# Short-convolution additions and the product with v issued to GpSimd instead of VectorE, with another table of order moves

## Chip, cores and metric

The kernel runs on one core of a Trainium2 chip. The metric is the device time of one launch in microseconds (us), lower is better. Engines are named as in the profile: PE (TensorE matmul), PEld (its weight loads), DVE (VectorE), ACT (ScalarE), POOL (GpSimd), SP (the queue that issues most DMAs).

## What is computed

Two kinds of layer alternate over a sequence of 2048 tokens with 640 channels, in float32. A is a gated convolution layer, B a two-matrix ReLU layer; each adds to the residual.

```python
def _A_ref(q, k, v, shift_k, ssm_k, ssm_D):
    for t in range(4):                       # short causal convolution, per channel
        k_shift = k_shift + k_pad[:, t:t + S, :] * shift_k[:, 3 - t]
    kv = k_shift * v
    y = long_causal_convolution(kv, ssm_k)   # per channel, by FFT in the reference
    return q * (y + kv * ssm_D)
x = x + _A_ref(_layernorm(x), ...)
x = x + relu(_layernorm(x) @ w1) @ w2        # 640 -> 1728 -> 640
```

The same A and B are applied twice (A, B, A, B) with the same k, v and weights, so y is computed once and used twice.

## The kernel before, in words

The sequence is cut into 8 chunks of 256 tokens. The long convolution is done chunk by chunk in a transformed domain. The work is cut into 21 units; a unit is two blocks of 128 channels (or one, for the last block of chunks 0 and 1) of one chunk or of two chunks. `transform` prepares a unit: it loads k, v and the filter, makes the four taps of the short convolution, adds them into the tile `acc`, multiplies `acc` with v (L729), forms sums and differences `sd` (L731, L732), transposes them on PE (L801) and multiplies them with a cosine matrix (tiles `pr`, `pg`). The results (`at`, `gt`) are spilled to memory for later chunks. `products` multiplies transformed chunks with transformed filters (L920 into `pd` or `pacc`, L925 adds them up), and PE transforms back (tile `pq`). The layer-norms, the residual and the two matrix products per chunk and layer are in `prep` and `main`; a main is one chunk and layer of 256 tokens, except in chunks 0 and 1, where it is half a chunk. In `main` PE makes `h` (L1461 to L1464), ACT applies the ReLU (L1604), DVE forms the low half `hl` (L1605), and PE multiplies both halves with w2 (L1433 to L1436).

The taps. In the first three units, all of chunk 0, a DVE instruction multiplies and adds in one (L708, L719). In the other 18 units ACT writes a scaled tap into a buffer `tp`, of which there are two (L651), and an addition `acc <- acc, tp` follows (L725), three times per unit. The product with v is at L729 in all 21 units.

Which engine runs an elementwise step with a name is decided by the tuple `ONPOOL`: a step whose name is in it goes to GpSimd, any other to VectorE.

```python
def gps(n, fn, reads, writes, prio):
    plan.op("POOL", 0.15 + n * 0.0021, fn, reads, writes, prio)
def ew(k, n, fn, reads, writes, prio):
    if k in ONPOOL:
        gps(n, lambda: fn(POOL), reads, writes, prio)
    else:
        dve(n, lambda: fn(DVE), reads, writes, prio)
```

The order on every engine is made ahead of time by `Plan`: a list scheduler that gives each step a cost and a priority, picks on each engine the ready step of best priority, and repeats this with keys that the table `MOVES` disturbs. What comes out is a fixed sequence per engine; on the chip each engine runs its own in order and waits where an input is late. GpSimd has little in its queue before: constants at the start, and 40 accumulating DMAs later (L673 adds `hr` to the filter tile `gs`; L786 makes the third part of `at` and `gt`).

Of the kernel before, what the change touches and what calls it, by code (L numbers as in the profile page):

```python
# [60 lines left out]
    (696239, 0.5, 108, 1308, 100), (709771, 15, 448, 848, 30), (757111, 1, 108, 118, 1000), (501689, 2, 206, 216, 1000), (793993, 2, 337, 737, 300), (75396, 2, -13, 137, 300),  # L61
    (827797, 0.2, 700, 850, 300), (811472, 0.5, -596, 604, 30), (617709, 4, 132, 532, 30), (809540, 1, 194, 594, 100), (987377, 4, 212, 362, 100), (205444, 2, 45, 195, 10),
    (511112, 2, 487, 547, 1000), (877225, 0.5, -33, 117, 300), (117084, 0.5, 145, 1345, 30), (392551, 8, -154, 246, 30), (228520, 2, 569, 969, 10), (284008, 8, -67, 1133, 10),
    (718585, 8, 678, 738, 30), (888747, 8, 287, 297, 1000), (962148, 1, -66, 1134, 30), (296808, 4, 510, 570, 300), (465037, 4, 78, 88, 1000), (771820, 0.5, 54, 114, 1000),
    (450406, 2, 321, 381, 300), (193537, 15, 214, 274, 3), (390307, 15, -131, 269, 10), (245960, 2, 317, 717, 30), (135498, 0.5, 639, 789, 300), (838399, 2, -31, 119, 30),
    (360983, 0.2, 554, 704, 1000), (762403, 4, 691, 751, 100), (938671, 8, 327, 477, 10), (89728, 4, -473, 727, 10), (53109, 4, 519, 544, 300), (356850, 0.5, 379, 779, 100),
    (50293, 0.2, -60, 1140, 300), (819375, 8, 99, 159, 30), (379115, 0.5, 382, 782, 100), (93648, 1, 680, 705, 1000), (398170, 1, 336, 486, 300), (829260, 8, 97, 497, 10),
    (707274, 15, 550, 700, 30), (415872, 0.5, -400, 800, 30), (727371, 1, 318, 378, 1000), (130652, 1, 379, 779, 30), (7433, 8, 107, 1307, 10), (559442, 4, 770, 795, 300),
    (621464, 0.2, 120, 1320, 100), (859335, 2, 72, 132, 100), (385222, 4, -58, 92, 100), (385554, 1, -208, 992, 30), (907221, 15, -2, 148, 30), (379287, 8, 337, 347, 300),
    (661111, 1, 156, 1356, 30), (909741, 4, 503, 903, 3), (697842, 1, -509, 691, 30), (89717, 0.5, 279, 339, 1000), (280960, 15, 440, 500, 100), (679836, 0.2, 571, 721, 100),  # L70
    (372502, 8, -207, 193, 30), (458612, 8, 109, 259, 30), (86548, 2, 537, 597, 300), (884426, 8, 814, 839, 30), (434125, 0.5, 499, 649, 100), (315057, 2, -68, 1132, 10),
    (730170, 4, 229, 629, 30), (126174, 0.5, -435, 765, 30), (190559, 8, 740, 750, 300), (255787, 1, 223, 373, 100), (722617, 15, 603, 753, 10), (21533, 4, 637, 787, 30),
    (280667, 1, 192, 217, 1000), (789770, 1, -605, 595, 100), (519538, 1, 274, 674, 100), (973148, 1, -605, 595, 30), (800972, 2, 392, 417, 1000), (816430, 2, 86, 236, 30),
    (391026, 4, 193, 218, 30), (486292, 2, 462, 487, 1000), (96439, 1, 408, 468, 1000), (453822, 4, 463, 613, 100), (905038, 4, -235, 965, 10), (934931, 0.5, 456, 856, 100),
    (379448, 15, 110, 135, 30), (847180, 8, 639, 789, 30), (651893, 8, 191, 341, 10), (974932, 0.2, -333, 867, 100), (898605, 8, 814, 874, 100), (328450, 0.5, 272, 332, 1000),
    (798154, 2, 143, 168, 100), (712104, 15, 472, 872, 10), (912566, 8, 568, 628, 100), (271480, 4, 37, 437, 10), (978163, 15, 327, 387, 100), (427782, 4, -183, 217, 30),
    (277854, 8, 79, 229, 30), (116122, 1, 42, 1242, 30), (253383, 0.5, -391, 809, 30), (622704, 2, 399, 459, 1000), (954265, 1, -25, 1175, 10), (867752, 8, 92, 242, 3),
    (390094, 0.2, 472, 872, 1000), (476637, 8, 573, 633, 100), (169012, 15, 299, 359, 30), (691903, 0.5, 435, 585, 1000), (646340, 0.5, -130, 1070, 30), (448317, 4, 84, 144, 100),
    (242667, 8, 722, 782, 30), (72971, 1, 737, 797, 300), (706991, 2, 238, 388, 100), (555710, 0.2, 15, 165, 1000), (9127, 1, 134, 1334, 100), (326956, 4, 177, 1377, 3),
    (307605, 1, -144, 1056, 30), (139482, 8, 303, 328, 300), (72000, 4, 291, 351, 100), (53081, 8, 129, 529, 3), (894170, 1, -58, 1142, 30), (451873, 2, 275, 675, 30),  # L80
    (115506, 15, 181, 1381, 10), (224945, 4, 48, 108, 30), (421425, 0.2, -6, 144, 1000), (381049, 4, 705, 765, 100), (497728, 1, -46, 354, 100), (543923, 8, 755, 905, 3),
    (536244, 2, 605, 755, 100), (953119, 2, 78, 138, 30), (676870, 15, 43, 68, 30), (372928, 15, -23, 377, 3), (605775, 15, 172, 182, 100), (30852, 4, 43, 1243, 10),
    (836145, 1, 121, 521, 100), (583412, 2, 508, 533, 1000), (752286, 0.2, 60, 460, 100), (353978, 15, 181, 241, 30), (607191, 15, 433, 583, 30), (874516, 4, 315, 375, 100),
    (661545, 8, -141, 259, 3), (508993, 15, 44, 194, 10), (920832, 2, 513, 913, 30), (157791, 8, 822, 882, 300), (527839, 0.5, -2, 148, 100), (376321, 1, 325, 725, 100),
    (928893, 2, 722, 782, 100), (205389, 15, 669, 729, 30), (166129, 15, 668, 1068, 10), (200362, 15, 178, 1378, 3), (552466, 4, 2, 152, 30), (763892, 0.5, 115, 140, 1000),
    (490494, 15, 597, 747, 30), (907558, 0.5, 392, 792, 30), (160270, 4, 393, 543, 100), (779627, 2, 443, 503, 300), (803556, 15, 140, 540, 10), (518039, 8, 503, 563, 100),
    (232112, 1, 122, 1322, 10), (902345, 2, -354, 846, 30), (9895, 1, 571, 631, 1000), (366264, 15, 65, 90, 30), (936527, 15, 293, 693, 3), (79619, 4, -169, 231, 30),
    (370231, 15, 518, 668, 30), (971813, 8, 488, 888, 10), (357754, 8, 312, 322, 1000), (237151, 2, 590, 740, 100), (305234, 15, 379, 404, 30), (754176, 2, 349, 749, 30),
    (418234, 8, 383, 408, 100), (105563, 1, 220, 1420, 30), (39099, 0.5, -595, 605, 30), (617760, 4, 143, 153, 300), (462015, 1, -177, 223, 100), (561869, 15, 759, 819, 3),
    (867484, 1, 491, 516, 1000), (792807, 0.5, 165, 565, 300), (893093, 8, -282, 918, 3), (961195, 0.5, 272, 422, 300), (780129, 2, 23, 48, 1000), (215859, 2, 290, 440, 100),  # L90
    (57360, 4, 427, 577, 30), (129201, 4, 623, 683, 300), (320957, 4, 316, 376, 100), (924052, 4, 450, 600, 30), (167525, 8, 361, 511, 100), (140874, 15, 265, 275, 300),
    (477116, 0.2, 95, 1295, 100), (107592, 8, 219, 279, 30), (671450, 2, 81, 106, 100), (121218, 1, -143, 1057, 30), (807461, 15, 494, 554, 100), (100199, 4, 247, 397, 30),
    (645106, 8, 479, 504, 3), (967239, 8, 249, 309, 30), (599905, 4, -178, 222, 30), (130555, 4, 339, 739, 10), (636712, 15, 594, 744, 10), (186050, 8, -324, 876, 10),
    (632646, 4, 303, 363, 100), (717447, 15, 289, 314, 100), (837830, 8, 146, 296, 3), (286728, 1, -33, 1167, 30), (513363, 4, 448, 598, 30), (515689, 15, 110, 1310, 3),
    (731992, 2, 151, 551, 30), (883402, 2, 136, 1336, 30), (375061, 15, 464, 614, 30), (475228, 2, -64, 1136, 30), (289290, 4, -475, 725, 10), (447762, 4, 122, 132, 1000),
    (889528, 0.5, 240, 1440, 100), (802878, 15, 447, 847, 10), (300829, 2, 576, 726, 100), (115977, 2, 572, 632, 300), (542977, 15, 762, 912, 10), (481545, 4, 507, 657, 100),
    (272913, 8, -107, 293, 10), (458051, 4, 302, 312, 1000), (855640, 15, 254, 314, 30), (554685, 0.5, -477, 723, 30), (873255, 4, 304, 454, 30), (247105, 4, 208, 268, 100),
    (120225, 8, 356, 506, 30), (35554, 2, 373, 398, 300), (836984, 2, -604, 596, 30), (47715, 1, -372, 828, 30), (274188, 15, -423, 777, 3), (510639, 8, 629, 779, 30),
    (422172, 1, 412, 472, 1000), (766593, 4, 276, 336, 100), (233761, 8, 6, 31, 1000), (759964, 4, 154, 1354, 30), (597972, 1, 233, 1433, 100), (191352, 0.2, 195, 345, 1000),
    (703329, 8, 745, 805, 30), (638523, 15, 474, 624, 3), (993091, 2, 550, 700, 100), (333553, 15, 477, 502, 30), (583499, 2, 768, 793, 100), (53434, 8, 298, 308, 300),  # L100
    (408119, 0.2, -319, 881, 100), (982891, 2, 716, 776, 100), (960677, 1, -20, 130, 100), (83885, 8, 761, 771, 100), (533065, 2, 303, 328, 300), (192995, 8, 707, 857, 30),
# [108 lines left out]
ONPOOL = ()  # L210
# [1626 lines left out]
```

## Time and profile before

| | us |
|---|---|
| median of 3 runs | 846.0 (845.83 to 849.47) |
| the profiled execution, its own time | 850.39 |
| its span, first to last instruction | 848.6 |
| PE busy | 836.8 |
| DVE busy | 778.7 |
| ACT busy | 518.3 |
| POOL busy | 43.8 |

The profiled execution is 4.4 us above the median, and 1.8 us of its time lies outside the span. The granted TensorE clock was 0.998 on average. Matmuls overlap in the record, so a busy PE is not by itself a PE at its peak.

### The profile page before, as it was taken

How to read it: one execution, taken by the hardware profiler on the slowest of the kernel's cores; microseconds unless marked ns; L12 is line 12 of the kernel's file. 1: busy time of each engine (PE TensorE's matmuls, PEld its weight loads, DVE VectorE, ACT ScalarE, POOL GpSimd, SP SyncE). 2: the span in 40 equal slices, each digit the busy share in tenths (PEclk: the TensorE clock that was granted, in tenths of full speed). 3: DMA queues.
4: the chain of work that ended last, by engine and by line, in shares of the span. 5: the costliest groups of instructions: out<-in, count | busy, mean ns of one | idle time of the engine just before them, and what ended most of it. 6: DMA issues, size and time to landing. Idle time of an engine off the chain costs nothing.

```text
span 848.6 us, 20004 instructions
## 1 busy us (share of the span) xinstructions
PE 836.8 (99%) x7937; PEld 668.0 (79%) x7937; DVE 778.7 (92%) x1404; ACT 518.3 (61%) x1233; POOL 43.8 (5%) x54
## 2 busy tenths in 40 slices
PE   8999999999998999999999999999999999999998
PEld 6987878888877778777787777777777788888886
DVE  6999999999998899999999999999797799988676
ACT  5798588456784576646657375555515386867531
POOL 0000000000001011011010101010100000000000
PEclk9999999999999999999999999999999999999999
DMA  8995868986989889796997959598977466051200
GB/s 296 394 325 201 266 185 257 313 282 177 314 260 264 277 233 285 233 286 180 226 300 210 260 173 225 164 194 250 247 254 245 115 211 151 22 140 26 58 33 32
DMA packets 138000, 181.68 MB, mean 214 GB/s; under 512 B 53809, under 2 KB 95537, under 8 KB 137906
## 3 DMA queue, kind: packets, MB, share of 16 engines
q1 hardware_dynamic: 129586, 169.91, 65.3%
q0 software_dynamic: 8320, 10.49, 8.3%
q8 instruction: 62, 1.02, 0.5%
q14 instruction: 32, 0.26, 0.1%
HBM read 124.59 MB, written 34.08 MB: 187 GB/s over the span
## 4 chain that ended last, share of the span: by engine, by line
PE 70%; DVE 19%; DMA 4%; ACT 3%; issue 2%; SPq 1%; DVEq 0%; POOLq 0%; ACTq 0%
PE h L1461 8%; PE h L1462 8%; PE h L1464 8%; PE o L1434 6%; PE o L1433 6%; PE o L1384 6%; PE o L1436 6%; PE h L1449 3%; DVE pd L920 3%; DVE pacc L925 3%; PE oc L1433 2%; PE oc L1434 2%; PE pg L754 2%; PE h L1451 1%; PE oc L1436 1%
## 5 line engine op out<-in xcount | busy, mean ns | idle before, releaser
L1461 PE MATMUL h<-xT,w 128*128 128x256 f16 (+1 forms) x1030 | 237.1, 250 | 0.7 <-DVE hl L1610 0.4
L1462 PE MATMUL h<-xT,w 128*128 128x256 f16 (+1 forms) x1030 | 237.0, 250 | 0.0
L1464 PE MATMUL h<-xT,w 128*128 128x256 f16 (+1 forms) x1030 | 237.0, 250 | 0.0
L1433 PE MATMUL o<-w,hh 128*128 128x512 f16 x336 | 127.3, 379 | 0.0
L1434 PE MATMUL o<-w,hh 128*128 128x512 f16 x336 | 127.3, 379 | 0.0
L925 DVE TENSOR_TENSOR pacc<-pacc,pd 128x1536 f32<-128x1536 f32 (+1 forms) x75 | 123.3, 1643 | 0.5
L1462 PEld LDWEIGHTS <-w 128*128 128x128 f16 x1130 | 110.6, 98 | 15.9 <-issue 0.9
L1461 PEld LDWEIGHTS <-w 128*128 128x128 f16 x1130 | 110.5, 98 | 14.7
L1464 PEld LDWEIGHTS <-w 128*128 128x128 f16 x1030 | 100.8, 98 | 6.7
L1604 ACT ACTIVATE hh<-h 128x512 f16<-128x512 f32 (+1 forms) x97 | 46.8, 483 | 71.2 <-PE h L1464 40.3
L1433 PEld LDWEIGHTS <-hh 128*128 128x128 f16 x672 | 65.7, 98 | 29.0
L1434 PEld LDWEIGHTS <-hh 128*128 128x128 f16 x672 | 65.8, 98 | 28.2
L920 DVE TENSOR_TENSOR pd<-Ax,Gx 128x768 f32<-128x768 f32 x83 | 78.1, 949 | 6.7 <-DMA Gx<-G 6.6
L1436 PE MATMUL o<-w,hl 128*128 128x512 f16 x208 | 78.8, 379 | 0.0
L1433 PE MATMUL oc<-w,hh 128*128 128x128 f16 x336 | 73.8, 220 | 0.0
L1434 PE MATMUL oc<-w,hh 128*128 128x128 f16 x336 | 73.6, 219 | 0.0
L1436 PEld LDWEIGHTS <-hl 128*128 128x128 f16 x416 | 40.7, 98 | 25.1 <-DVE hl L1605 0.6
L1449 PE MATMUL h<-xT,w 128*128 128x256 f16 (+1 forms) x400 | 57.4, 251 | 2.2 <-DMA xT<-xh 2.2
L651 ACT ACTIVATE tp<-kt,shs 128x256 f32<-128x256 f32 (+1 forms) x78 | 43.6, 575 | 18.9 <-DVE acc L725 17.2
L1436 PE MATMUL oc<-w,hl 128*128 128x128 f16 x208 | 45.6, 219 | 0.4 <-DVE hl L1605 0.4
L920 DVE TENSOR_TENSOR pd<-at,Gx 128x768 f32<-128x768 f32 x46 | 43.0, 950 | 0.7 <-DMA Gx<-G 0.5
L1449 PEld LDWEIGHTS <-w 128*128 128x128 f16 x400 | 36.3, 98 | 7.8 <-issue 2.5
(276 smaller groups left out, 1974.8 us busy)
## 6 DMA issues: line engine op xcount, KB each, us to landing
Ax<-A SPq DMA_DIRECT2D x89, 384.0 KB, 4.2
Gx<-G SPq DMA_DIRECT2D x89, 384.0 KB, 4.3
G<-gt SPq DMA_DIRECT2D x14, 768.0 KB, 5.0
A<-at SPq DMA_DIRECT2D x14, 768.0 KB, 5.7
ws<-in_w SPq DMA_DIRECT2D x28, 320.0 KB, 6.5
y<-Y SPq DMA_DIRECT2D x22, 320.0 KB, 4.7
x<-in_q SPq DMA_DIRECT2D x16, 320.0 KB, 5.7
gs<-in_hF SPq DMA_DIRECT2D x20, 256.0 KB, 4.7
```

What stands on the lines that cost most here:

```text
L651: ACT.activation(o[:, i : i + m], kview(i, m, j), AF.Copy, scale=shs[:, t, j : j + 1])
L920: ew(f"mac{j % POOLMOD}", 768, lambda e, x=dst[i], av=av, gv=gv: e.tensor_mul(x.t, av(), gv()), [ax, gx], [dst[i]], pr_)
L925: dve(768 * (hi - lo), lambda lo=lo, hi=hi, pd=pd: DVE.tensor_add(acc[:, lo:hi], acc[:, lo:hi], pd[:, lo:hi]), [*sums[lo:hi], *dst[lo:hi]] ...
L1384: PE.matmul(b[:, c : c + w], x, y[:, z : z + w], start=done[i] == 1, stop=end, skip_group_check=fin)
L1433: PE.matmul(z, hh[:, c], wh[:, d], start=(j == JS[0] and i == 0 and (h == 0 or s == S[0])), stop=False)
L1434: PE.matmul(z, hh[:, c], wl[:, d], start=False, stop=end and tail)
L1436: PE.matmul(z, hl[:, c], wh[:, d], start=False, stop=end)
L1449: PE.matmul(p[:, z], wh, xv(t, x), start=b and x == 0, stop=e and x == 1)
L1461: PE.matmul(p[:, z], wh, xv(t, 0), start=b, stop=False)
L1462: PE.matmul(p[:, z], wh, xv(t, 1), start=False, stop=tail and e)
L1464: PE.matmul(p[:, z], wl, xv(t, 0), start=False, stop=e)
L1604: act(2 * R, lambda pv_=pv_, hh=hh: ACT.activation(hh.t, pv_(), AF.Relu), [src], [hh], URGENT)
```

## The change

Two edits. `ONPOOL` gets four names, so that the three tap additions and the product with v are issued to GpSimd; and `MOVES` is another table (693 moves before, 800 after, of which 448 are in both; two of its lines are shown).

```diff
-ONPOOL = ()
+ONPOOL = ("tap1", "tap2", "tap3", "kv")
...
-    (696239, 0.5, 108, 1308, 100), (709771, 15, 448, 848, 30), (757111, 1, 108, 118, 1000), (501689, 2, 206, 216, 1000), (793993, 2, 337, 737, 300), (75396, 2, -13, 137, 300),
+    (696239, 0.5, 108, 1308, 100), (709771, 15, 448, 848, 30), (757111, 1, 108, 118, 1000), (793993, 2, 337, 737, 300), (75396, 2, -13, 137, 300), (617709, 4, 132, 532, 30),
```

75 instructions change engine: 54 tap additions (18 units by three) and 21 products with v. The product with v goes over in the first three units too; only their taps stay on VectorE. Code lines below the table stand 18 lines further down after the change, so L725, L729, L731 become L743, L747, L749.

DVE at the start of the program, first unit, before (acc is the convolution of unit 0, sd its sums and differences, the next acc that of unit 1):

```order
L708 SCALAR_TENSOR_TENSOR acc_0_200<-kt_0_174,shs,acc_0_200 128x256 x6
L729 TENSOR_TENSOR acc_0_200<-acc_0_200,vt_0_190 128x512
L731 TENSOR_TENSOR sd_0_232<-acc_0_200 128x256
L732 TENSOR_TENSOR sd_0_232<-acc_0_200 128x256
L719 SCALAR_TENSOR_TENSOR acc_2_230<-kt_2_192,shs,acc_2_230 128x256 x3
```

The same place on DVE after the change:

```order
L726 SCALAR_TENSOR_TENSOR acc_0_200<-kt_0_174,shs,acc_0_200 128x256 x6
L749 TENSOR_TENSOR sd_0_237<-acc_0_200 128x256
L737 SCALAR_TENSOR_TENSOR acc_2_230<-kt_2_192,shs,acc_2_230 128x256
L750 TENSOR_TENSOR sd_0_237<-acc_0_200 128x256
L737 SCALAR_TENSOR_TENSOR acc_2_230<-kt_2_192,shs,acc_2_230 128x256
```

The product is gone from DVE, so its next instruction, the sum into sd, now needs GpSimd's result, and the second unit's taps are spread around it.

DVE in the last main of half a chunk, before; pd, pacc and Ax, Gx belong to the products of earlier units, gl to a filter, hh to PE's next input:

```order
L920 TENSOR_TENSOR pd_3_2_4333<-Ax_3_1_4_4300,Gx_3_2_4_4322 128x768
L1605 SCALAR_TENSOR_TENSOR hh_2_4467<-h_2_4399,hh_2_4467 128x256
L725 TENSOR_TENSOR acc_1_4330<-acc_1_4330,tp_1_4265 128x512
L925 TENSOR_TENSOR pacc_3_4274<-pacc_3_4274,pd_3_2_4333 128x1536
L1191 RECIPROCAL stdB_0_0_4514<-stdB_0_0_4514 128x2
L1605 SCALAR_TENSOR_TENSOR hh_3_4512<-h_3_4451,hh_3_4512 128x256
L1000 TENSOR_TENSOR ys_1_4536<-pq_1_4494,qs_1_4524 128x256
L999 TENSOR_TENSOR ys_1_4536<-pq_1_4494,qs_1_4524 128x256
L763 TENSOR_TENSOR gl_0_4547<-gs_0_3905,gh_0_4534 128x512
L763 TENSOR_TENSOR gl_0_4580<-gs_0_3946,gh_0_4538 128x512
L920 TENSOR_TENSOR pd_3_4_4582<-Ax_3_2_3_4380,Gx_3_1_3_4416 128x768
L725 TENSOR_TENSOR acc_1_4330<-acc_1_4330,tp_1_4522 128x512
```

The same main on DVE after the change:

```order
L1623 SCALAR_TENSOR_TENSOR hh_2_4654<-h_2_4592,hh_2_4654 128x256
L781 TENSOR_TENSOR gl_1_4686<-gs_1_4113,gh_1_4612 128x512
L1623 SCALAR_TENSOR_TENSOR hh_3_4684<-h_3_4637,hh_3_4684 128x256
L781 TENSOR_TENSOR gl_1_4709<-gs_1_4164,gh_1_4633 128x512
L943 TENSOR_TENSOR pacc_0_4431<-pacc_0_4431,pd_0_4_4496 128x1536
L1209 RECIPROCAL stdB_0_0_4733<-stdB_0_0_4733 128x2
L938 TENSOR_TENSOR pd_0_6_4745<-Ax_0_3_0_4475,Gx_0_2_0_4386 128x768
L938 TENSOR_TENSOR pd_0_6_4745<-Ax_0_3_0_4475,Gx_0_1_0_4525 128x768
```

The additions to acc are gone, and the row is as full as it was: products and filter steps stand here one unit earlier than before (products of unit chunk 4/5 block 0 where those of chunk 3 blocks 3 and 4 stood, and gl of the unit after it).

GpSimd's queue around the third unit of chunks 4 and 5, after the change (gs<-hr, gt and at are accumulating DMAs, the rest additions to acc and its product with vt). Before, this queue held only the DMA rows:

```order
L804 DMA gt_0_4131<-gt_0_4131 128x2x256
L691 DMA gs_1_4113<-hr_1_4024 128x512
L743 TENSOR_TENSOR acc_2_4123<-acc_2_4123,tp_2_4335 128x512
L691 DMA gs_1_4164<-hr_1_4024 128x512
L804 DMA at_0_4362<-at_0_4362 128x2x256
L743 TENSOR_TENSOR acc_2_4123<-acc_2_4123,tp_2_4447 128x512
L743 TENSOR_TENSOR acc_2_4123<-acc_2_4123,tp_2_4477 128x512
L747 TENSOR_TENSOR acc_2_4123<-acc_2_4123,vt_2_4331 128x512
L804 DMA gt_1_4807<-gt_1_4807 128x2x256
```

DMA issues and additions now share one queue, and an addition that waits for its tap holds back the DMA behind it.

Counted over the whole DVE row list up to the `hl` row of the first j of main 12 (chunk 4, first layer): before, 19 of the 21 units have their `sd` rows ahead of it and 123 multiplications (L920, with the eight of L881) stand there; after the change all 21 units and 140 multiplications do.

242 rows, old and new, of the table MOVES are left out of this document.

## The prediction

> **What bounds the kernel now.** First the page's busy times: PE is the engine that is never free, DVE comes next, POOL does almost nothing.
>
> ```profile
> PE 836.8 (99%) x7937; PEld 668.0 (79%) x7937; DVE 778.7 (92%) x1404; ACT 518.3 (61%) x1233; POOL 43.8 (5%) x54
> ```
>
> An average hides stages, so next the busy time by stretch (span and then PE, PEld, DVE, ACT, POOL, granted clock, DMA share, GB/s).
>
> ```profile
> 0.00:45.00 45.00, 41.02 (x330) 36.69 (x331) 35.90 (x98) 28.77 (x67) 1.81 (x14) 0.96 0.95 343
> 100.00:300.00 200.00, 197.10 (x2193) 158.91 (x2191) 191.39 (x328) 130.80 (x331) 8.15 (x8) 1.00 0.87 262
> 300.00:600.00 300.00, 299.55 (x2482) 229.73 (x2481) 297.33 (x437) 178.55 (x423) 31.50 (x30) 1.00 0.87 231
> 600.00:800.00 200.00, 199.70 (x1798) 160.92 (x1796) 168.00 (x355) 121.38 (x288) 2.38 (x2) 1.00 0.52 146
> 800.00:849.00 49.00, 44.46 (x522) 37.81 (x520) 31.95 (x86) 12.47 (x26) 0.00 (x0) 1.00 0.09 32
> ```
>
> From 300 to 600 us both PE (299.55 of 300) and DVE (297.33 of 300) are full. DVE has room only after 600, when the convolution is over. PE's idle time is 4.0 us at the start, 2.9 + 0.45 + 0.3 in the middle and 4.5 in the tail. Third, how much PE can bear if DVE is late: one `hl` and PE's use of it.
>
> ```profile
> 445.05 0.68 DVE L1605 SCALAR_TENSOR_TENSOR hl<-h,hh 128x512 f16<-128x512 f32 x1
> ...
> 445.79 0.22 PE L1436 MATMUL oc<-w,hl 128*128 128x128 f16 x1
> ```
>
> DVE finishes hl at 445.73, PE reads it at 445.79: a margin of 0.06 us. PE did not wait there, but a DVE that is late by a microsecond makes PE late by about as much, and a PE that is always busy never makes it up. So the question is not how much work DVE loses, but whether DVE keeps to its fixed order.
>
> **What the change removes from DVE.** The four groups that move, with busy time and mean:
>
> ```profile
> L725 DVE TENSOR_TENSOR acc<-acc,tp 128x512 f32<-128x512 f32 x51 | 34.9, 683 | 2.0 <-ACT tp L651 1.2 <-ACT acc L651 0.8
> L729 DVE TENSOR_TENSOR acc<-acc,vt 128x512 f32<-128x512 f32 x19 | 12.9, 681 | 0.1
> L725 DVE TENSOR_TENSOR acc<-acc,tp 128x256 f32<-128x256 f32 x3 | 1.3, 417 | 0.0
> L729 DVE TENSOR_TENSOR acc<-acc,vt 128x256 f32<-128x256 f32 x2 | 0.8, 412 | 0.0
> ```
>
> 34.9 + 12.9 + 1.3 + 0.8 = 49.9 us of busy time in 75 instructions. Neighbours overlap a little, so one of 512 columns frees less than 683 ns:
>
> ```profile
> 442.37 0.68 DVE L960 TENSOR_TENSOR u<-u,pacc 128x512 f32<-128x512 f32 x1
> 442.97 0.68 DVE L973 TENSOR_TENSOR ul<-u,uh 128x512 fp32r<-128x512 f32 x1
> ```
>
> Starts lie 0.60 us apart, so some 44 us of DVE time become free. PE's own work does not change: the same matmuls run. The most that freed DVE time can give PE is the idle time in the middle, 3.65 us.
>
> **What the order does with it.** The order rows show that the room is spent at once: up to main 12 DVE has 140 multiplications and 21 transforms ahead where there were 123 and 19. 17 multiplications and eight more of the long additions (55 rows for 47, L925) are worth, by
>
> ```profile
> L920 DVE TENSOR_TENSOR pd<-Ax,Gx 128x768 f32<-128x768 f32 x83 | 78.1, 949 | 6.7 <-DMA Gx<-G 6.6
> L925 DVE TENSOR_TENSOR pacc<-pacc,pd 128x1536 f32<-128x1536 f32 x65 | 113.8, 1750 | 0.5
> ```
>
> 17 x 0.95 + 8 x 1.75 = 30 us, and two transforms' other rows make up most of the rest. So up to main 12 DVE is about as full as before, and it falls behind its order by whatever the additions on GpSimd cost it. PE also has two more transforms ahead of main 12. One of their matrix steps, its first and last of twelve matmuls and what follows:
>
> ```profile
> 459.66 0.36 PE L577 MATMUL pg<-gh,cGh 128*128 128x256 f32 x1
> ...
> 461.04 0.28 PE L579 MATMUL pg<-gh,cGl 128*128 128x256 f32 x1
> 461.17 0.28 PE L1461 MATMUL h<-xT,w 128*128 128x256 f16 x1
> ```
>
> takes 1.5 us. With the like step for `pr` and the transposes (some 0.4 us) a transform is 3.5 us of PE, two are 7 us: by so much PE comes to main 12 later on its own account, and so much lateness of DVE costs nothing.
>
> **What it adds.** 75 instructions on POOL. No row of before shows a tensor-by-tensor instruction there. The nearest are a copy with one input and a bare start:
>
> ```profile
> 1.66 0.29 POOL L547 CAST ident<-ident 128x128 f16<-128x128 f32 x1
> 1.89 0.09 POOL L554 MEMSET epst<- 128x1 f32 x1
> ```
>
> (0.29 - 0.09) / 127 = 1.5 ns a column for one input. For 512 columns that gives 0.09 + 0.8 = 0.9 us if a second input is free, 1.7 us if it doubles the time. I take 1.2, near the middle: 70 x 1.2 + 5 x 0.7 = 88 us of POOL, beside 44 busy now, spread over some 500 us. POOL does not become the bound. One unit's four steps take 4.8 us in a row, and a unit comes every 25 us or so.
>
> What decides is what an addition on POOL costs DVE while it runs. Both engines would read two SBUF tensors at once, and no row of before shows that. The bounds: nothing (0 us), or the whole 1.2 us in which DVE stands still. A gain below nothing is excluded, since DVE's own share is already taken off above. How much of DVE could be held up: between 300 and 600 us these rows
>
> ```profile
> L925 DVE TENSOR_TENSOR pacc<-pacc,pd 128x1536 f32<-128x1536 f32 x37 | 64.7, 1750 | 0.2
> L920 DVE TENSOR_TENSOR pd<-Ax,Gx 128x768 f32<-128x768 f32 x54 | 50.7, 948 | 0.1
> L1605 DVE SCALAR_TENSOR_TENSOR hl<-h,hh 128x512 f16<-128x512 f32 x35 | 23.9, 682 | 1.4 <-ACT hh L1604 1.4
> ...
> L1619 DVE SCALAR_TENSOR_TENSOR hh<-hb,hh 64x256 f16<-64x256 f32 x6 | 2.5, 418 | 0.2
> ```
>
> show the pattern: L925, L920 and most others take both inputs from SBUF, while L1605 takes one (h is in PSUM). The nine groups with an input in PSUM, of which L1605 is the first and L1619 the last, sum to 62 of 297 us, so about four fifths of DVE's time has two SBUF inputs. I take 0.68 us per addition of 512 columns, 0.42 of 256, the price of the row that is nearest, the same addition on DVE: the engines then do these additions at the joint cost that they have now, but the order counts them as free. It lies between 0 and 1.2.
>
> [...]
>
> **Edits that I cost by themselves.** *The start.* In the first unit the product stands between the taps and `sd`, and PE waits for what follows:
>
> ```profile
> 8.79 0.69 DVE L729 TENSOR_TENSOR acc<-acc,vt 128x512 f32<-128x512 f32 x1
> 9.52 0.43 DVE L731 TENSOR_TENSOR sd<-acc 128x256 f32<-128x256 f32 x1
> 10.09 0.68 PE L801 MATMUL pt<-ident,sd 128*128 128x128 f32 x4 [0.74 <-ACT gt L757]
> ```
>
> With 1.2 for 0.69 and two handovers, sd comes 0.5 to 1 us later; I add 1. This is also the new wait of the change: `sd` on DVE waits for POOL, and behind it in DVE's queue stand taps, multiplications and the next `hl`, for which PE waits. In later units the order leaves other rows between the last tap and `sd`; I take 0 there, and 18 x 1 = 18 us, were each as late as the first, as the other end. *POOL's DMAs.* They now stand behind additions:
>
> ```profile
> L673 POOL DMA_DIRECT2D gs<-hr x20 | 18.5, 925 | 401.0 <-DVE hh L1605 219.2 <-DMA gs<-in_hF 92.3 <-ACT hr L672 33.5
> ```
>
> POOL waited 401 us ahead of these 20, so an addition ahead delays a filter tile by 1 to 2 us that its unit mostly has; I take 0, covered by the matmuls of the main, and 2.6 us if that cover is gone: as much as PE idles where these DMAs first come,
>
> ```profile
> 250.00:300.00 50.00, 47.42 (x433) 36.58 (x431) 45.05 (x64) 28.59 (x68) 6.27 (x6) 1.00 0.98 265
> ```
>
> once more. *SP's queue.* Its loads wait for DVE to free their buffers:
>
> ```profile
> SPq L907 <- DVE pd L920: 112.2, 57, 5.7
> ```
>
> A later DVE makes them later by the same amount, not by more: 0.
>
> **The sum.** Additions beside DVE: 49.9 (70 and 5 at DVE's own prices). Start: +1. Taken off: 7 for PE's own later arrival, and 6, about half of the 8.6 + 2.7 us that DVE idles between 100 and 600 us. 49.9 + 1 - 7 - 6 = +38 us. The profiled execution of 850.39 us would become 888; it lies 4.4 above the median, so from the median **846.0 + 38 = 884 us**.
>
> **Rivals.**
> - *Full exclusion.* Every DVE instruction with two SBUF inputs stands still while POOL works: 1.2 x 4/5 = 0.96 us for each of 70, half for five: 70 us, so 70 + 1 - 13 = +58, **904 us**. For it: nearly all DVE rows are of that kind and DVE has no gap. Against it: a one-input instruction such as L1605 can fill part of the time. With 1.7 us per addition it would be 1.36 x 70 + 3 - 12 = +86, 932 us. Chance 0.2.
> - *Cheap.* A price of 0.2 to 0.4 us gives 15 to 30 us, less 13 plus 1: +3 to +18, **849 to 864 us**. Chance 0.14.
> - *Not slower: the engines do not disturb each other.* At a price under 13 / 75 = 0.17 us, DVE keeps to its order, and the 3.65 us that PE idles in the middle (2.6 of them between 250 and 300 us) can close: 846 - 3.6 = **842 us**. More needs a shorter start or tail, of which the order shows nothing on DVE's side but the moved product. For it: no row shows a disturbance. Against it: the two engines would have to read four streams at once at full rate. Chance 0.17; in 0.06 of it the new order also saves at the start or tail.
> - *The change does not do what it says.* The order shows all 75 instructions on POOL, and the products of the first three units with them. Chance 0.
>
> **How the numbers follow.** The forecast (price 0.4 to 0.85, 864 to 896) has 0.49. About 0.5% (4 us) is what a measurement of this kernel can tell from no change. Faster by more: 0.06. Within: 0.17 - 0.06 = 0.11, and 0.01 of the cheap case: 0.12. Slower: 0.82. The range from 845 to 915 leaves out the faster cases and half of those of no change (0.12) and the upper part of full exclusion (0.06).
>
> **What the profile after would show.** DVE's L920 and L925 longer than 949 and 1750 ns on average, or gaps on DVE, wherever POOL is busy: by 0.6 us or so per addition. POOL's additions at 0.9 to 1.7 us, more if they wait for DVE. PE with idle time on DVE (`hl`, `sl`, `u`) between 100 and 550 us, where it had almost none. DVE with more room after 500 us. If L920 stays at 949 and PE waits for nothing, the forecast is wrong, and the time is near 842. If PE waits for POOL's `acc` by way of `sd`, the price was not contention but the chain.

## The result and the profile after

The changed kernel takes **907.65 us** (median of 5 runs, 903.27 to 909.6) against 845.83 us before (5 runs, 844.66 to 849.47). The ratio is **1.0694, with a 95% interval of 1.067 to 1.0719**; 1.0694 is 59 us of 846; the two medians by themselves lie 62 us apart, and I go by the ratio below. The profiled execution is the fastest of the five: 903.27 us, with a span of 901.5. I had forecast 884 in a range of 845 to 915.

First the changed kernel's busy times by engine, from its page:

```profile
PE 850.2 (94%) x7937; PEld 669.5 (74%) x7937; DVE 799.7 (89%) x1329; ACT 520.0 (58%) x1233; POOL 168.0 (19%) x129
```

DVE has 75 instructions fewer than before and is busy for 21 us longer. PE's share falls from 99% to 94%: in a span that is 52.9 us longer, it is idle for 51.3 us (901.5 - 850.2) instead of 11.8. The other 13.4 us stand as busy time of PE, with the same 7937 matmuls; a lower granted clock (0.994 over the execution against 0.998) makes some 3 of them, by an estimate from that share, and the rest is not resolved here. POOL's 124 us more are its 75 additions.

The chain of work that ended last, by engine, shows whom the end now hangs on:

```profile
PE 45%; DVE 42%; issue 6%; ACT 4%; DMA 2%; POOL 1%; SPq 1%; DVEq 0%; ACTq 0%; POOLq 0%
```

Before, PE held 70% of this chain and DVE 19%. POOL itself, which does the work that was moved, is 1% of it.

The changed kernel's busy times by stretch (columns as in the prediction) tell where:

```profile
45.00:100.00 55.00, 47.17 (x508) 36.43 (x506) 52.13 (x90) 39.83 (x82) 15.32 (x11) 1.00 0.74 241
100.00:300.00 200.00, 181.23 (x2057) 145.06 (x2056) 194.96 (x291) 124.59 (x320) 61.33 (x39) 1.00 0.85 256
300.00:500.00 200.00, 186.52 (x1489) 139.69 (x1488) 195.79 (x253) 107.47 (x241) 61.16 (x46) 0.97 0.89 231
...
600.00:800.00 200.00, 200.00 (x1703) 155.02 (x1702) 157.06 (x298) 118.72 (x286) 2.38 (x2) 1.00 0.53 148
```

While POOL adds (61 us in the second and the third row), PE is idle for 7.8, 18.8 and 13.5 us, and from 100 us on DVE is nearly full. In the first of these stretches PE had no idle time before:

```profile
45.00:100.00 55.00, 55.00 (x623) 43.91 (x621) 54.09 (x106) 46.32 (x101) 0.00 (x0) 1.00 0.78 251
```

Once the additions are over, PE is full again. The granted clock is 0.97 from 300 to 500 us, where before had 1.00 from 100 us on.

What did DVE's own instructions do? These groups of DVE, by tile and shape, have the same code and the same operands as before:

```profile
L943 DVE TENSOR_TENSOR pacc<-pacc,pd 128x1536 f32<-128x1536 f32 x65 | 119.1, 1833 | 0.8
L938 DVE TENSOR_TENSOR pd<-Ax,Gx 128x768 f32<-128x768 f32 x83 | 80.9, 982 | 3.2 <-DMA Gx<-G 3.0
L938 DVE TENSOR_TENSOR pd<-at,Gx 128x768 f32<-128x768 f32 x46 | 49.0, 1080 | 0.4
L938 DVE TENSOR_TENSOR pacc<-Ax,gt 128x768 f32<-128x768 f32 x35 | 38.3, 1111 | 0.2
L858 DVE TENSOR_TENSOR at<-at 128x512 f32<-128x512 f32 x9 | 11.3, 1250 | 0.0
L1623 DVE SCALAR_TENSOR_TENSOR hl<-h,hh 128x512 f16<-128x512 f32 x49 | 33.4, 685 | 13.5 <-ACT hh L1622 13.5
```

The first two had 1750 and 949 ns on average. All but the last read two tensors in SBUF, and all of those have grown. `hl`, whose input `h` lies in PSUM, has 685 ns where it had 683. A mean hides that a few instructions grow by much. Single rows of DVE, and then of POOL, from the changed kernel's timeline (start, duration):

```profile
62.85 1.76 DVE L858 TENSOR_TENSOR at<-at 128x512 f32<-128x512 f32 x1
...
67.13 0.95 DVE L938 TENSOR_TENSOR pacc<-Ax,gt 128x768 f32<-128x768 f32 x1
...
69.79 1.82 DVE L938 TENSOR_TENSOR pd<-at,Gx 128x768 f32<-128x768 f32 x1
```

```profile
62.37 3.36 POOL L743 TENSOR_TENSOR acc<-acc,tp 128x512 f32<-128x512 f32 x2 [17.11 <-ACT tp L669]
68.97 1.84 POOL L743 TENSOR_TENSOR acc<-acc,tp 128x512 f32<-128x512 f32 x1 [3.24 <-ACT tp L669]
```

Between two POOL additions, at 67.13, a multiplication L938 takes its usual 0.95 us. Beside one, at 69.79, the same kind takes 1.82. I set each of DVE's rows against the median of its own form before: 64 are longer by more than 0.2 us, together by 56.4 us. Over all rows the differences sum to **58.6 us**, which is 0.78 us for each of the 75 additions; a kernel without the additions (below) gives 1.9 us by the same sum, so 56 to 59 us are stretch. 36 of the 64 are longer by 0.95 to 1.1 us. The 34 rows of L1623 and L1694, with one input in PSUM and one in SBUF, that overlap an addition have grown by 0.01 us at most.

POOL's additions, by shape, are stretched as well:

```profile
L743 POOL TENSOR_TENSOR acc<-acc,tp 128x512 f32<-128x512 f32 x51 | 85.3, 1673 | 188.0 <-ACT tp L669 89.4 <-ACT acc L669 38.4 <-DVE sl L840 23.8
L747 POOL TENSOR_TENSOR acc<-acc,vt 128x512 f32<-128x512 f32 x19 | 34.4, 1813 | 11.7 <-DVE acc L726 6.5 <-DVE acc L737 3.9
```

The shortest of this size took 1.26 us. Last, what PE waits for in the changed kernel (total, times, longest):

```profile
PE h L1479 <- DVE hh L1623: 5.4, 8, 1.6
PE oc L1454 <- DVE hl L1623: 5.0, 4, 2.4
```

These are two of many such waits. In this list PE waits some 32 us for DVE (1.3 before) and some 10 for ACT (2 before). DVE's `hl` and `hh` come late, though their own rows have not grown. They stand in DVE's fixed order behind rows that have.

### The profile page after: what moved, and what is told of

It reads as the page before. It is cut to its first block, busy times and chain, and to the rows that moved or that the text cites. A ratio compares the mean times of both kernels' runs of the same rounds, so it can differ in the third digit from the quotient of the medians.

```text
span 901.5 us, 20063 instructions
## 1 busy us (share of the span) xinstructions
PE 850.2 (94%) x7937; PEld 669.5 (74%) x7937; DVE 799.7 (89%) x1329; ACT 520.0 (58%) x1233; POOL 168.0 (19%) x129
## 3 DMA queue, kind: packets, MB, share of 16 engines
q8 instruction: 62, 1.02, 0.4%
## 4 chain that ended last, share of the span: by engine, by line
PE 45%; DVE 42%; issue 6%; ACT 4%; DMA 2%; POOL 1%; SPq 1%; DVEq 0%; ACTq 0%; POOLq 0%
PE o L1402 8%; DVE pd L938 8%; DVE pacc L943 7%; PE h L1479 5%; PE h L1480 5%; PE h L1482 5%; PE o L1451 3%; PE o L1452 3%; PE o L1454 3%; DVE pacc L938 2%; PE h L1467 2%; DVE w L1112 2%; DVE ul L991 1%; DVE hh L1623 1%; DVE x L1278 1%
## 5 line engine op out<-in xcount | busy, mean ns | idle before, releaser
L943 DVE TENSOR_TENSOR pacc<-pacc,pd 128x1536 f32<-128x1536 f32 (+1 forms) x75 | 134.3, 1791 | 0.9
L1480 PEld LDWEIGHTS <-w 128*128 128x128 f16 x1130 | 110.7, 98 | 29.5 <-issue 13.2
L1479 PEld LDWEIGHTS <-w 128*128 128x128 f16 x1130 | 110.8, 98 | 24.5 <-issue 5.1
L743 POOL TENSOR_TENSOR acc<-acc,tp 128x512 f32<-128x512 f32 (+1 forms) x54 | 90.4, 1674 | 200.2 <-ACT tp L669 90.6
L1482 PEld LDWEIGHTS <-w 128*128 128x128 f16 x1030 | 100.9, 98 | 6.9
L938 DVE TENSOR_TENSOR pd<-Ax,Gx 128x768 f32<-128x768 f32 x83 | 80.9, 982 | 3.2 <-DMA Gx<-G 3.0
L669 ACT ACTIVATE tp<-kt,shs 128x256 f32<-128x256 f32 (+1 forms) x78 | 43.9, 576 | 27.9 <-POOL acc L743 27.6
L938 DVE TENSOR_TENSOR pd<-at,Gx 128x768 f32<-128x768 f32 x46 | 49.0, 1080 | 0.4
```

Of the source, the lines that this page charges most:

```text
L743: ew(f"tap{j}", w, lambda e, tp=tp: e.tensor_add(acc.t, acc.t, tp.t), [acc, tp], [acc], pr_)
L938: ew(f"mac{j % POOLMOD}", 768, lambda e, x=dst[i], av=av, gv=gv: e.tensor_mul(x.t, av(), gv()), [ax, gx], [dst[i]], pr_)
L943: dve(768 * (hi - lo), lambda lo=lo, hi=hi, pd=pd: DVE.tensor_add(acc[:, lo:hi], acc[:, lo:hi], pd[:, lo:hi]), [*sums[lo:hi], *dst[lo:hi]] ...
L1479: PE.matmul(p[:, z], wh, xv(t, 0), start=b, stop=False)
L1480: PE.matmul(p[:, z], wh, xv(t, 1), start=False, stop=tail and e)
L1482: PE.matmul(p[:, z], wl, xv(t, 0), start=False, stop=e)
```

## The experiments

Three theories stood at the start. **Port** (a name and no more: no run shows what the two engines share): an addition on GpSimd that reads SBUF holds up a DVE instruction that reads two tensors there. **Queue**: not the data but the hand-overs cost; DVE and ACT wait for GpSimd's results and buffers, and GpSimd's DMAs wait behind its additions. **Order**: the new table of moves is slower by itself. Kernels that were run together share the runs of the kernel before, whose medians were 847.88 us (the first four), 848.05 (the next four) and 848.5 (the last four).

### The additions left out, the order kept

```diff
-            gps(n, lambda: fn(POOL), reads, writes, prio)
+            gps(n, lambda: None, reads, writes, prio)
```

> The order of the changed kernel on every engine, but the 75 additions and products on GpSimd are not issued at all (so the taps 1 to 3 and the product with v are left out of the result); everything else is the same. Theory 'port': GpSimd's instructions hold up DVE, so without them DVE keeps to its order: 839 to 850 us, L920 and L925 back at 950 and 1750 ns, PE idle about 10 us. Theory 'queue': the additions come too slowly for what waits for them; that goes too, so the same 839 to 850 us. Theory 'order': the new table of moves made a worse order; then 865 us or more are left.

Measured: **858.0 us** (855.39 to 861.68), ratio 1.0127 [1.0094, 1.0161]. The same groups of DVE in this kernel:

```profile
L943 DVE TENSOR_TENSOR pacc<-pacc,pd 128x1536 f32<-128x1536 f32 x65 | 113.9, 1752 | 0.8
L938 DVE TENSOR_TENSOR pd<-at,Gx 128x768 f32<-128x768 f32 x46 | 43.1, 951 | 0.4
```

Neither expectation is met: the time lies between 850 and 865 us. Nothing is stretched; DVE is busy for 743.6 us, 56.1 less than in the changed kernel. So the 59 us fall into two parts. The new order costs 1.0127, about 10 us, with no addition anywhere. The presence of the additions on GpSimd costs the other 48 (0.0567 of 846). PE is idle for 17.5 us of this kernel's span (856.8 - 839.3), 5.7 more than before. Its longest waits (left out is one of 2.0 us at the very start, which the kernel before has too):

```profile
PE h L1480 <- DMA xT<-xh: 2.1, 1, 2.1
PE h L1467 <- DMA xT<-xh: 2.1, 1, 2.1
...
PE pt L819 <- DVE sd L750: 1.7, 1, 1.7
```

Two loads of `xT` come late from 100 to 300 us, where the DMA share is 0.97 (0.87 before), and the first `sd` is late at the start. But one load came late in the kernel before too:

```profile
PE h L1449 <- DMA xT<-xh: 2.2, 1, 2.2
```

so the loads explain some 2 us of the 10 at most. Waits for DVE, most of them under 1 us, grow from 1.3 to 6.6 us. What in the order makes them was not tried, nor whether the fuller DMA queues delay the loads.

### GpSimd as busy, but only writing

```diff
+    class Stand:
+        def do(o, x, y):
+            for z in (o, y, o):
+                POOL.memset(z, 0.0)
+        tensor_add = tensor_mul = do
...
-            gps(n, lambda: fn(POOL), reads, writes, prio)
+            gps(n, lambda: fn(Stand), reads, writes, prio)
```

> The order of the changed kernel; each of the 75 instructions on GpSimd is replaced by three memsets that write acc, then tp (or vt), then acc, so GpSimd is busy about 3 x 0.52 = 1.56 us at each place (1.26 us is the shortest addition of the changed kernel, 1.70 the mean) and is waited for as before, but reads nothing from SBUF. The convolution is left out of the result. Theory 'port' (DVE's second input and GpSimd's reading exclude each other): 839 to 855 us, DVE rows not stretched. Theory 'queue': GpSimd is as slow for those who wait as in the changed kernel: 890 to 910 us.

Measured: **857.73 us** (857.24 to 861.19), ratio 1.013 [1.0104, 1.0156], the same as with nothing there, and 3 us above the range, in which the order's 10 us were not counted. Its busy times by engine, and one DVE group:

```profile
PE 840.5 (98%) x7937; PEld 668.5 (78%) x7937; DVE 744.5 (87%) x1329; ACT 519.7 (60%) x1233; POOL 151.8 (18%) x279
```

```profile
L946 DVE TENSOR_TENSOR pd<-at,Gx 128x768 f32<-128x768 f32 x46 | 43.1, 951 | 0.4
```

POOL is nearly as busy as in the changed kernel (151.8 us for 168.0), in the same order, with the same hand-overs to and from DVE and ACT, and it costs nothing. So the hand-overs as such are not what costs, and the queue theory falls in the form stated. One thing is not the same: ACT waits longer for GpSimd in the changed kernel, where the additions are stretched (its line first, then that of this kernel).

```profile
ACT tp L669 <- POOL acc L743: 27.6, 18, 3.8
ACT tp L677 <- POOL tp L547: 9.2, 11, 2.7
```

What this adds to PE's waits for ACT (some 10 us there, 2 here) no run separates from the hold-up of DVE.

### GpSimd reading one tensor

```diff
+            for _ in range(2):
+                POOL.tensor_copy(o, y)
```

This stands in place of the three memsets: two copies for each addition.

> The order of the changed kernel; each of the 75 instructions is replaced by two copies of tp (or vt) into acc on GpSimd, each with one SBUF input, some 2 x 0.85 us by the copy of 128 columns (so taps are copied over each other instead of added). Theory 'port' in the form that any reading on GpSimd excludes DVE's second input: GpSimd reads 1.7 us at each place instead of 1.26, so 900 to 930 us, L920 and L925 stretched by up to 0.9 us at a time, more often than in the changed kernel. In the form that only two inputs on GpSimd do: 840 to 855 us. Theory 'queue': 895 to 910 us.

Measured: **894.42 us** (890.99 to 896.89), ratio 1.0551 [1.0516, 1.0587]. Again one group of DVE:

```profile
L946 DVE TENSOR_TENSOR pd<-at,Gx 128x768 f32<-128x768 f32 x46 | 44.6, 984 | 0.4
```

76 rows of DVE are longer by more than 0.2 us, nearly all by 0.3 to 0.4, together by 29 us (32 over all rows). The time is 6 us under the range that I gave for this. So it is GpSimd's reading that holds DVE up (L946 at 984 ns here, at 951 beside memsets), and with one input already, in smaller pieces. Here the time grew by 36 us over the two kernels without reads, somewhat more than the rows.

### The same order, the additions issued on DVE

```diff
-            gps(n, lambda: fn(POOL), reads, writes, prio)
+            gps(n, lambda: fn(DVE), reads, writes, prio)
```

> The order of the changed kernel, but the 75 instructions are issued to VectorE at the places at which that order issues them to GpSimd: DVE carries 49.9 us (44 us with neighbours overlapping) that the order does not count. Theory 'port': what counts is DVE time beyond the order; the stretched rows of the changed kernel sum to 59 us, here it is 44 to 50, so less late: 875 to 895 us. Theory 'queue': GpSimd is out of the way: 842 to 855 us.

Measured: **888.28 us** (885.97 to 889.29), ratio 1.0476 [1.0448, 1.0504]. DVE is busy for 785.6 us, 42.0 more than without the additions, and POOL for 44.0. Nothing is stretched (L938 951 ns, L943 1752). With the very order that was made for GpSimd, the additions cost 30 us on DVE (888.28 - 858.0) and 48 on GpSimd. The move takes 42 us off DVE and puts 56 of hold-up on it.

### The two engines alone

A kernel of its own, which leaves out the reference's computation. Each block lets GpSimd and DVE (or ACT) run instructions without dependence on each other, after a common start:

```python
for i in range(16): POOL.tensor_add(f[i % 2], d, e)      # 128x512; then copy, memset
for i in range(40): DVE.tensor_add(c[i % 2], a, b)       # 128x768; then one input in PSUM, or tensor_scalar
```

> A kernel of its own without the computation: GpSimd additions of 512 columns (two SBUF inputs) alone (line 44); DVE additions of 768 columns from SBUF alone (47); both together (50 and 52); GpSimd additions beside DVE additions with one input in PSUM (55 and 57); GpSimd memsets beside DVE additions from SBUF (61 and 63); GpSimd copies with one input beside DVE additions from SBUF (66 and 68); GpSimd additions beside DVE tensor-scalar with one SBUF input (71 and 73); beside ACT (76 and 78). Theory 'port': GpSimd 1.26 us alone, DVE 0.95; together both take turns, DVE at 0.95 + 1.1 about 2.0 us for each that meets an addition; with PSUM input DVE keeps 0.69; beside memsets DVE keeps 0.95; beside copies it is stretched; beside ACT nothing. Theory 'queue': DVE at 0.95 everywhere.

Its groups: first each engine by itself, then both together, then with one input of DVE in PSUM, with memsets, with copies, and with a one-input instruction on DVE.

```profile
L44 POOL TENSOR_TENSOR f<-d,e 128x512 f32<-128x512 f32 x10 | 12.3, 1274 | 9.1 <-DVE d L40 9.1
L47 DVE TENSOR_TENSOR c<-a,b 128x768 f32<-128x768 f32 x16 | 14.0, 950 | 0.0
```

```profile
L50 POOL TENSOR_TENSOR f<-d,e 128x512 f32<-128x512 f32 x16 | 30.8, 1963 | 16.3 <-DVE d L40 16.3
L52 DVE TENSOR_TENSOR c<-a,b 128x768 f32<-128x768 f32 x40 | 51.9, 1371 | 0.0
L57 DVE TENSOR_TENSOR c<-pa,b 128x512 f32<-128x512 f32 x40 | 24.0, 678 | 0.0
L63 DVE TENSOR_TENSOR c<-a,b 128x768 f32<-128x768 f32 x32 | 28.3, 957 | 0.0
L68 DVE TENSOR_TENSOR c<-a,b 128x768 f32<-128x768 f32 x40 | 43.1, 1151 | 0.0
L73 DVE TENSOR_SCALAR c<-b 128x512 f32<-128x512 f32 x40 | 30.5, 839 | 0.0
L40 DVE TENSOR_SCALAR d<-g 128x512 f32<-128x512 f32 x9 | 3.8, 427 | 0.3
```

Together, 16 additions lengthen 40 DVE instructions by (1371 - 950) x 40 / 16 = **1.05 us per addition**, and are themselves stretched from 1.27 to 1.96 us. With an input in PSUM DVE takes 678 ns (additions of the same size from SBUF took 681 with GpSimd idle, L39), and beside memsets 957 ns for 950: no effect. A copy on GpSimd costs DVE (1151 - 950) x 40 / 20 = 0.40 us. The `TENSOR_SCALAR`, with one SBUF input, takes 839 ns instead of 427, 1.03 us per addition. The port theory holds, with its price.

### An order that knows the price

The planner is given a step of 0.8 us on DVE beside each addition, with the changed kernel's moves.

```diff
             gps(n, lambda: fn(POOL), reads, writes, prio)
+            plan.op("DVE", 0.8 * n / 512, lambda: None, reads[-1:], (), prio)
```

> The changed kernel, but the planner is told of the cost on DVE: beside each step on GpSimd it plans a DVE step of 0.8 us (0.4 for 256 columns) that issues nothing. So the order leaves DVE room for being held up. Theory 'port': DVE has 729 + 59 us of work that the order knows of, little more than before (779), so PE waits for DVE much less: 850 to 875 us. Theory 'queue': the additions are as slow as they were: 895 us or more.

Measured: **945.52 us** (943.55 to 946.87), ratio 1.1142 [1.1115, 1.117]: a clear miss. The added steps shift the numbers by which the moves address the plan, so that moves fall on other steps. With the additions left out of this kernel:

```diff
-            gps(n, lambda: fn(POOL), reads, writes, prio)
+            gps(n, lambda: None, reads, writes, prio)
```

> The order that was planned with room on DVE (945.52 us with the additions on GpSimd), and the 75 instructions not issued (taps 1 to 3 and the product with v are left out of the result). Theory 'port', with lateness against the order as what costs: 44 us are stretched there and the order has room for 59, so no more than 15 us come back: 930 to 945 us, and its time is that of a bad order. If room in the order does not help, 900 to 910 us.

it takes **919.7 us** (918.47 to 922.67), ratio 1.0856 [1.0821, 1.0891]. So this order is bad by 0.0856 of 848, or 73 us, before any hold-up. The hold-up itself is 26 us (945.52 - 919.7), with 50 rows longer by more than 0.2 us and 43.5 us over all rows: 0.59 of the stretch becomes time, where it is 48 / 58.6 = 0.82 in the changed kernel. I had expected 15 us at most. With room in the order the hold-up is weaker, but not gone; whether the room weakens it or the idle time that PE has in this bad order anyway (60.4 us without the additions), these runs do not tell.

### The product alone, and the old moves

Both start from the kernel before, with its own moves; only the tuple changes. First the product with v alone:

```diff
-ONPOOL = ()
+ONPOOL = ("kv",)
```

> The kernel before with its own moves, and only the 21 products with v on GpSimd. Theory 'port': 21 x 0.78 us = 16 us of hold-up, less about 5 that DVE's idle time takes: 855 to 864 us. Theory 'queue': three of the four steps of a unit are back on DVE and the chain on GpSimd is one step long: 846 to 850 us.

Measured: **882.79 us** (881.06 to 884.08), ratio 1.0402 [1.0371, 1.0433]. Then all four names:

```diff
-ONPOOL = ()
+ONPOOL = ("tap1", "tap2", "tap3", "kv")
```

> The four names on GpSimd with the table of moves of before. Theories 'port' and 'queue': as the changed kernel within 10 us, 895 to 920 us. Theory 'order': if the new table is what costs, 855 us or less.

Measured: **929.63 us** (924.86 to 930.78), ratio 1.0946 [1.0908, 1.0985]. Both are slower than I had expected. For the second I had thought that the changed kernel's own moves might be what costs; they are better by some 21 us (ratios 1.0946 and 1.0694). The misses left it open whether a hold-up per addition explains them, so each was run with the additions left out, by the edit shown above.

> The order of the kernel with only the product with v on GpSimd (882.79 us), and those 21 instructions not issued (the product with v is left out of the result). Theory 'port': the stretched DVE rows there sum to only 12 us, so at most 12 us come back: 870 to 880 us, and the rest of its distance to 848 is its order. If the hold-up is worth more than the stretched rows show, 850 us.

> The order of the four names on GpSimd with the old table of moves (929.63 us), and the 75 instructions not issued (taps 1 to 3 and the product with v are left out of the result). Theory 'port': the stretched rows there sum to 64 us, of which some 12 find room, as in the changed kernel (59 us stretched, 49 between 907 and 858): 875 to 885 us. If its distance to the changed kernel is hold-up too, 858 us; if all of it is order, 905 us or more.

Measured: **865.98 us** (863.87 to 867.66), ratio 1.0217 [1.0188, 1.0246], and **879.27 us** (876.65 to 882.08), ratio 1.0376 [1.0344, 1.0407]. The first is 4 us under its range. The hold-up is thus 50.4 us for 75 additions (66 rows longer by more than 0.2 us, 64.1 us over all rows) and 16.8 us for 21 products, 0.80 each (13 rows, 12.3 us over all). The 16.8 us are more than the stretch, and I had said at most 12. In that kernel DVE also waits for the product itself:

```profile
DVE sd L731 <- POOL acc L729: 6.8, 8, 1.4
```

In the changed kernel this wait is 2.1 us. So a hand-over that cost nothing in the one order may cost a few microseconds in another; that was not tried by itself. The rest, 17.5 and 31 us, is the order. A change of costs in the planner alone, without its own search of moves, costs tens of microseconds here, which is what made my expectations miss.

### What DVE's freed time is worth at best

The order of before, with the 75 additions left out on DVE and nothing put on GpSimd:

```diff
-            gps(n, lambda: fn(POOL), reads, writes, prio)
+            dve(n, lambda: None, reads, writes, prio)
```

> The kernel before with its own order and with the same 75 instructions not issued on DVE (taps 1 to 3 and the product with v are left out of the result): DVE is 50 us lighter, GpSimd does nothing more. PE is the bound, so at most its idle time of 3.65 us in the middle comes back: 842 to 847 us. If DVE were the bound, 810 to 830 us.

Measured: **847.75 us** (846.67 to 849.1, 10 runs), ratio 0.9995 [0.9982, 1.0007], just above the range. Its busy times by engine:

```profile
PE 835.9 (99%) x7937; PEld 667.3 (79%) x7937; DVE 742.9 (88%) x1329; ACT 518.1 (61%) x1233; POOL 43.8 (5%) x54
```

DVE is lighter by 36 us of busy time (778.7 to 742.9), and nothing comes of it: PE is full. In this order the move could have gained nothing that a measurement tells (1.5 us at most, by the interval), even if GpSimd had cost nothing.

## Why the prediction was right or wrong

**The sign and the mechanism were right.** PE bounds the kernel and gains nothing from a lighter DVE (the last experiment), and a DVE that is held up by GpSimd is late against its order, so that PE waits for `hl` and `hh`. What failed is the size: +38 forecast, +59 measured.

**The price per addition** was the term mis-sized first. I took 0.68 us, the price of the same addition on DVE, for a sum of 49.9. Measured were 58.6 us of stretch, 0.78 for each of the 75. It lies inside the band of 0.4 to 0.85 that I gave the forecast, so this is 9 of the 21 us that were missing. My reason for the value did not hold: I thought that the two engines would do the additions at the joint cost that they had on DVE. With the two engines alone, a meeting costs DVE 1.05 us, most of POOL's 1.27, and the average in the changed kernel is lower. 10 of the 75 additions overlap no lengthened row: beside most of them DVE ran small rows, rows with an input in PSUM, or nothing. One, of 256 columns, was itself the one held up: it took 3.65 us, where the shortest of its size took 0.72, beside L938, L811 and L943, none of which grew. How much of the difference each of these makes was not worked out.

**The new order** was the term that I did not have. I counted it as refilled room and gave it no price; it costs 10 us with no addition in it. The row counts showed that more work stood earlier, and I read that only as an absence of slack, not as a cost of its own.

**What is taken off** was about right: 7 + 6 = 13 us. Of 58.6 us of stretch 48 became time, so 11 were covered. Whether they were covered by PE's own later arrival and DVE's idle time, as I put it, no run separates.

**The start** (+1) was not needed: PE's waits for the first `sd` are 1.2 and 0.3 us in the changed kernel (its two rows) and 1.7 with the additions left out. The new wait of `sd` for GpSimd, of which I feared up to 18 us, occurs twice:

```profile
DVE sd L749 <- POOL acc L747: 2.1, 2, 1.4
```

**POOL's DMAs** at 0 were right: the memset kernel keeps POOL nearly as busy ahead of them and loses nothing by it. **SP's queue** was not tried by itself; PE waits 2.3 us for a DMA in the changed kernel and 2.2 before.

The measured parts are 48 us for the presence of the additions and some 11 for the order (0.0127 of 846), the 59 of the ratio. That 58.6 us of stretch less 11 give the 48 is no test, since the 11 are the difference of the two.

**The rivals.** *Full exclusion* gave 904 us and stands nearest to the time, but partly by accident: its mechanism comes near to what the two engines alone show beside additions (1.05 us a meeting, where an addition takes 1.27 alone), its price of 0.96 for every addition is too high (0.78), and the order's 10 us make up for that. *Cheap* and *not slower* fall with L938 at 1080 ns and L1623 unchanged. That rows of DVE with an input in PSUM are spared, which the four fifths took as given, is what the runs show: with the two engines alone, GpSimd's additions make 1371 ns of 950 where DVE has two SBUF inputs, and 678 ns stay where one input is in PSUM; memsets leave 957. That DVE stands still for the whole of GpSimd's instruction is not what the copies show: one takes 1.19 us alone and costs DVE 0.40.

**The profile after** was as I said it would look: L938 and L943 longer wherever POOL is busy, POOL's additions at 1.7 us under load, PE waiting on DVE. Room on DVE came later than I said, after 600 us and not after 500 (95.84 of 100 us busy from 500 to 600).

## What to carry to other kernels

An elementwise instruction that is moved from a full DVE to an idle GpSimd can hold up the engine that it was to free. Here each of the 75 took 0.56 us off DVE (42.0 us of busy time in all) and put 0.78 us back (58.6), where memsets in its place put nothing back (L946 at 951 ns); on another kernel this has to be measured. Before such a move, leave the instructions out where they stand: that kernel's time shows what the freed time is worth in that order, and here it was nothing. Where the order is computed from costs, run the new order with the moved work left out as well, since its own cost (10 us here, up to 73 with moves that no longer fit) is otherwise put down to the engine.

## What the runs showed of the hardware that I had not expected

- A `TENSOR_SCALAR` of DVE with one SBUF input is held up as much as an addition with two: 839 ns for 427, 1.03 us per GpSimd addition (1.05 with two). In the changed kernel one `xc<-x,negmB` (L1288) was longer by 1.02 us as well (1.56 us for 0.54). The share of rows with two SBUF inputs, as I counted it, leaves this form out.
- A copy of 128x512 on GpSimd is hardly shorter than an addition, yet holds DVE up far less:

```profile
L59 POOL COPY f<-d 128x512 f32<-128x512 f32 x1 | 1.2, 1194 | 5.3 <-DVE d L40 5.3
L66 POOL COPY f<-d 128x512 f32<-128x512 f32 x20 | 25.5, 1327 | 14.0 <-DVE d L40 14.0
```

  1.19 us alone against 1.27 for the addition, but 0.40 us of hold-up against 1.05. Between these two, how long DVE is held up does not follow from how long GpSimd's instruction takes.
- GpSimd and ACT did not hold each other up: additions beside ACT's activations took 1.26 us (1.27 alone), and in the changed kernel ACT's taps of 512 columns (L669) took 718 ns, and 718 before.
- The granted clock was lower in three short stretches of the changed kernel, each right after one in which PE had been idle for more than half of the time. It was 0.50 for 3.41 us each, from 348.3, 420.0 and 474.6 us. Ahead of the second and in it:

```profile
416.59:420.01 3.42, 1.32 (x10) 0.55 (x9) 3.38 (x7) 3.13 (x6) 0.89 (x1) 1.00 0.67 265
420.01:423.42 3.41, 3.41 (x17) 2.02 (x16) 3.41 (x8) 0.00 (x0) 1.25 (x2) 0.50 0.88 123
```

  The trace's clock records give each of the three 3.413 us, and their starts lie 71.68 and 54.61 us apart, 21 and 16 times as much. Cut into such lengths, this trace has PE busy for 0.99, 1.31 and 1.34 us in the ones right ahead of the three, less than in any other while PE works; the next, two with 1.63 us, were followed by a clock of 1.00. In the kernel before, 1.63 us, from 9.49 us on, were followed by 0.50, so these numbers give no limit. Where the idle time was more spread out, 3.9 us of it from 125 to 150 us, the clock stayed at 1.00. Over the whole execution it was 0.994 against 0.998 before, by which I estimate some 3 us of PE's 840. No run tried this by itself.
